# Routing an attention output to experts: 32x32 block transposes on VectorE in place of TensorE transposes, and rows scattered in quarters

## The chip, the cores and the metric

One core of a Trainium2 chip runs the whole program. The metric is the time of one execution in device microseconds. The engines are named as the profile names them: PE is TensorE (PEld its weight loads), DVE is VectorE, ACT is ScalarE, POOL is GpSimd, SP is SyncE.

## The reference

Squared-ReLU attention without a softmax, whose gated output goes token by token to one of eight experts.

```python
batch, seq, d_model, d_qk = 8, 2496, 256, 64          # attention
N, D, E, F = 19968, 256, 8, 1024                      # experts; N = 8 * 2496

scores = (1 / S) * z @ z.T                            # per batch
attn = np.maximum(scores, 0) ** 2
x = (u * (attn @ v)).reshape(N, D)

logits = x @ w_gate                                   # N x 8
e_idx = argmax(logits)                                # first of equals
probs = exp(logits - max); probs /= probs.sum() + 1e-9
gate_w = probs[e_idx]
eom = 1 / (1 + exp(-(x @ w_output_gate)))             # N x 8
for e in range(E):
    mask = e_idx == e
    h = np.maximum(x[mask] @ w1[e], 0)                # 256 -> 1024
    out[mask] = gate_w[mask] * eom[mask, e] * (h @ w2[e])   # 1024 -> 256
```

## The kernel before, in words

**Precision.** Every operand is kept as two float32r parts, a high part (a cast) and a low part (the operand minus its cast), and a product is two or three matmuls. So each operand needs a cast (ACT or DVE) and a subtraction (DVE).

**Attention.** The loop `for k, (b, c, jp) in enumerate(units)` runs over 8 batches, 5 chunks of columns `c` (512 wide, chunk 0 is 448) and 10 pairs `jp` of key blocks, one unit each. `make` prepares a unit two ahead (`LOOK = 2`): `scores` computes a block of the squared scores (matmuls at L200 and L201, ReLU at L202, square at L205, cast to `ah` at L207 on ACT for odd `jp` and at L209 on DVE for even, subtraction `al` at L211), and stores its transpose (DVE, L223 to L229) for later use; `take` fetches a transposed block that an earlier chunk stored (cast L255, subtraction L259). Chunk 0 has ten `scores` units and later chunks have ever more `take` units. `weigh` multiplies with `v` (twelve matmuls, L274) and accumulates two PSUM tiles `o` over the ten units.

**The tail.** When a chunk's ten units are done, a `Tail` finishes it: one call of `advance` in each unit of the next chunk, `TAIL = 11` steps, in this order. `gate` (DVE: times `u`), `split` (casts L314 on ACT, subtractions L315 on DVE), `rows(0)` and `rows(1)` (each: four PE transposes against an identity, L355, and two ACT copies out of PSUM, L364, into `xt`, four blocks of 128 tokens with 258 values each), `logits` (four matmuls with 32 weight columns, L325, an ACT copy `lg`, and for chunk 0 a POOL memset of the unused columns, L332), `turn` (four PE transposes, L338, an ACT copy `lt`), `choose` and `pick` (small DVE operations on 128 partitions x 4 blocks x 8 experts: the maximum, a one-hot row, a running count), `factor` and `finish` (gate weight and token number into the last two columns of `xt`), `place` (three small matmuls that count earlier tokens of the same expert) and `scatter` (small DVE operations that give the row index, then four indirect DMAs from POOL, L471, of 128 rows each, into the DRAM tensor `xs`, which has a region for each expert). PSUM bank `mp` (one buffer) serves all of the tail's PE results. The last tail has no next chunk: its steps are called from the list `later` during the first expert slots.

**Experts.** `Slot`s of 512 tokens (32 of them) and of 256 follow. A slot's table entry gives its expert and first row in `xs`. `load_x` reads the rows in four DMAs of 256-byte pieces, `turn` (DVE, L718) brings them into columns, `split_x` splits them, `split_w` splits the weights (L711 on ACT, L712 on DVE), `up` (L752, ReLU L761, L762) and `down` (L779) compute, and `down` writes `y` and scatters it to the output (POOL, L788). `then` is called after each of a slot's twelve parts (eight in `up`, four in `down`) and takes one entry of `later`. The first slots are cut so that they hold only tokens of the first seven batches, so they do not wait for the last batch's scatters.

**Order.** Each engine runs its instructions in the order in which the program writes them (`manual_schedule`). Tiles of one tag share its buffers, and a new tile waits for the last reader of the buffer that it is given.

Of the kernel before, what the change touches and what calls it, by code (L numbers as in the profile page):

```python
# [8 lines left out]
F32 = mybir.dt.float32  # L9
# [30 lines left out]
TAIL = 11  # L40

WARM = 10
ROW = D + 2
# [4 lines left out]
def attention_moe(ctx, tc, zt, zq_in, ut, v, wg, w12, out):  # L48
# [13 lines left out]
    xs = dram.tile([E * CAP + TW, ROW], F32, name="xs")  # L62
# [6 lines left out]
    ident = const.tile([P, P], F32, name="ident")  # L69
    make_identity(nc, ident)  # L70
    upper = const.tile([P, P], BF16, name="upper")
    nc.gpsimd.affine_select(
        out=upper, in_=ones, pattern=[[1, P]], compare_op=ALU.is_gt, fill=0.0, base=0, channel_multiplier=-1
    )
    ramp_i = const.tile([P, E], I32, name="ramp_i")
# [4 lines left out]
    tok_i = const.tile([P, 2, 4], I32, name="tok_i")  # L80
    nc.gpsimd.iota(tok_i[:, 0], pattern=[[P, 4]], base=0, channel_multiplier=1)
    for k in range(4):
        nc.gpsimd.iota(
            tok_i[k * 32 : (k + 1) * 32, 1],
            pattern=[[32, 4]],
            base=P * k,
            channel_multiplier=1,
        )
    tok0 = const.tile([P, 2, 4], F32, name="tok0")
    nc.vector.tensor_copy(out=tok0, in_=tok_i)  # L90
    scan_mask = const.tile([P, E, 5], BF16, name="scan_mask")
# [3 lines left out]
    for k in range(2):  # L95
        h = const.tile([P, E, 5], BF16, name=f"hot{k}")
        nc.vector.memset(h, 0.0)
        hot.append(h)
# [91 lines left out]
    def scores(b, c, jp):  # L190
# [15 lines left out]
        if jp % 2:  # L206
# [78 lines left out]
    class Tail:  # L285
# [33 lines left out]
        def logits(self):  # L319
            w = self.w  # L320
            lp = ps_m.tile([P, CH], F32, name="mp")
            k = 0
            for xx in (self.xl, self.xh):
                for d in range(2):
                    nc.tensor.matmul(  # L325
                        out=lp[0 : 4 * E, :w], lhsT=wg_r[:, d], rhs=xx[:, d, :w], start=k == 0, stop=k == 3
                    )
                    k += 1
            lg = pool.tile([4 * E, CH], F32, name="lg", bufs=1)
            nc.scalar.copy(out=lg[:, :w], in_=lp[0 : 4 * E, :w])  # L330
            if w < CH:
                nc.gpsimd.memset(lg[:, w:CH], 0.0)  # L332
            self.lg = lg

        def turn(self):
            tp = ps_m.tile([P, CH], F32, name="mp")
# [657 lines left out]
```

## Time and profile before

| | before |
|---|---|
| median of 3 runs | 2325.96 us (2324.8 to 2327.41) |
| profiled execution, its own time | 2326.99 us |
| its span | 2325.3 us |
| PE busy | 2301.2 us, 99% |
| DVE busy | 1629.2 us, 70% |
| ACT busy | 1499.9 us, 65% |
| POOL busy | 341.5 us, 15% |
| DMA traffic | 345.87 MB, mean 149 GB/s |

The span is what the profiler recorded from the first instruction to the last; the execution's own time is 1.7 us longer. The attention takes the first 1380 us, about 170.6 us a batch, and the experts the rest, 22.4 us for a slot of 512 tokens and 11.5 us for one of 256. An engine's busy time is the union of its instructions; matmuls are pipelined and their ends are modelled, so that neighbours overlap. In timelines a row gives the start, the duration, the engine, the line, the operation with output and inputs, and how many were merged.

### The profile page before, as it was taken

Reading aid. Unit: us, or ns where it says so; the run is one execution under the profiler, and the core shown is the slowest. Engines: PE = TensorE matmul, PEld = TensorE weight load, DVE = VectorE, ACT = ScalarE, POOL = GpSimd, SP = SyncE. Lnnn points to the kernel's source line nnn. Section 1 sums busy time; section 2 is a strip of 40 time slices with the busy share of each in tenths; the row PEclk is TensorE's granted clock in tenths of the full one; section 3 lists DMA queues with packets and bytes.
Section 4 is the critical chain, followed back from the end, with each engine's and each line's share of the span. In section 5 each row is a group of like instructions: output and inputs, shape, how many; then the busy total and the mean of one; then the engine's idle time right before and its main releaser. Section 6 shows DMA issues by size and latency. Waiting matters only on the chain.

```text
span 2325.3 us, 38469 instructions
## 1 busy us (share of the span) xinstructions
PE 2301.2 (99%) x12786; PEld 1992.8 (86%) x12786; DVE 1629.2 (70%) x2785; ACT 1499.9 (65%) x2503; POOL 341.5 (15%) x353
## 2 busy tenths in 40 slices
PE   9999999999999999999999999999999999999997
PEld 7888888888888888888888879999999999999997
DVE  8778778778778778777778666656556565566775
ACT  8767677777767767677677664555545455555664
POOL 0011011111011111111111112121111211111111
PEclk9999999999999999999999999999999999999999
DMA  6684674675765756756755675313322234445331
GB/s 202 177 213 154 188 200 169 187 186 180 194 168 189 203 156 201 204 150 193 199 150 189 183 185 140 87 46 85 89 78 51 82 83 127 139 122 157 106 96 42
DMA packets 393916, 345.87 MB, mean 149 GB/s; under 512 B 133869, under 2 KB 320238, under 8 KB 393712
## 3 DMA queue, kind: packets, MB, share of 16 engines
q1 hardware_dynamic: 378288, 302.29, 47.3%
q0 software_dynamic: 15424, 41.08, 5.2%
q8 instruction: 102, 1.67, 0.3%
q14 instruction: 102, 0.84, 0.1%
HBM read 272.55 MB, written 128.37 MB: 172 GB/s over the span
## 4 chain that ended last, share of the span: by engine, by line
PE 55%; issue 32%; POOL 7%; DVE 2%; DMA 2%; ACT 1%; POOLq 0%; SPq 0%; DVEq 0%; ACTq 0%
PE o L274 43%; POOL out L788 7%; PE sc L200 5%; PE sc L201 4%; PE mp L325 1%; PE mp L355 1%; DMA xs<-xt,idx 1%; PE mp L338 1%; DMA z<-td 0%; POOLq L788 0%; DVE t L226 0%; ACT a L202 0%; DMA sx<-xs 0%; ACT a L205 0%; PE o L779 0%
## 5 line engine op out<-in xcount | busy, mean ns | idle before, releaser
L274 PE MATMUL o<-ah,v 128*128 128x512 f32 (+1 forms) x3200 | 974.7, 388 | 1.5 <-DVE v L172 1.2
L274 PEld LDWEIGHTS o<-ah,v 128*128 128x128 f32 x3200 | 596.6, 188 | 114.0 <-DVE v L172 4.2
L274 PE MATMUL o<-al,v 128*128 128x512 f32 (+1 forms) x1520 | 586.7, 386 | 0.0
L779 PE MATMUL o<-w,hh 128*128 128x256 f32 x2624 | 480.5, 283 | 0.0
L779 PEld LDWEIGHTS o<-w,hh 128*128 128x128 f32 x2624 | 412.9, 192 | 1.2
L712 DVE TENSOR_TENSOR w<-raw,w 128x512 fp32r<-128x512 f32 x400 | 269.3, 685 | 194.9 <-ACT w L711 194.9
L211 DVE TENSOR_TENSOR al<-a,ah 128x1024 fp32r<-128x1024 f32 (+1 forms) x232 | 274.4, 1183 | 184.3 <-ACT ah L207 174.2
L752 PE MATMUL sc<-xh,w 128*128 128x512 f32 (+1 forms) x1600 | 376.4, 352 | 0.5 <-ACT xh L728 0.5
L779 PE MATMUL o<-w,hl 128*128 128x256 f32 x1312 | 371.9, 283 | 0.9 <-DVE hl L762 0.9
L471 POOL DMA_INDIRECT xs<-xt,idx x160 | 176.1, 1100 | 1229.0 <-DVE u L304 618.9
L202 ACT ACTIVATE a<-sc 128x512 f32<-128x512 f32 (+1 forms) x480 | 252.5, 580 | 155.5 <-PE sc L201 155.5
L274 PEld LDWEIGHTS o<-al,v 128*128 128x128 f32 x1520 | 285.8, 188 | 53.4
L752 PEld LDWEIGHTS sc<-xh,w 128*128 128x128 f32 x1600 | 270.8, 190 | 38.5 <-ACT xh L728 0.6
L761 ACT ACTIVATE hh<-sc 128x512 fp32r<-128x512 f32 x328 | 196.4, 599 | 122.8 <-PE sc L752 122.7
L788 POOL DMA_INDIRECT out<-y,meta x164 | 161.3, 984 | 741.9 <-ACT y L787 736.5
L787 ACT ACTIVATE y<-o,meta 128x256 f32<-128x256 f32 x164 | 77.8, 474 | 294.9 <-issue 195.7
L779 PEld LDWEIGHTS o<-w,hl 128*128 128x128 f32 x1312 | 251.9, 192 | 2.3 <-DVE hl L762 1.1
L205 ACT ACTIVATE a<-a 128x1024 f32<-128x1024 f32 (+1 forms) x240 | 246.2, 1026 | 7.6
L762 DVE SCALAR_TENSOR_TENSOR hl<-sc,hh 128x512 fp32r<-128x512 f32 x328 | 224.2, 684 | 35.1 <-ACT hh L761 24.6
L711 ACT CAST w<-raw 128x512 fp32r<-128x512 f32 x400 | 239.8, 614 | 0.0
L752 PE MATMUL sc<-xl,w 128*128 128x512 f32 (+1 forms) x800 | 216.2, 352 | 0.5 <-DVE xl L729 0.5
L200 PE MATMUL sc<-z,hl 128*128 128x512 f32 (+1 forms) x480 | 193.2, 403 | 1.7 <-ACT a L202 0.9
(132 smaller groups left out, 2281.7 us busy)
## 6 DMA issues: line engine op xcount, KB each, us to landing
raw<-in_w SPq DMA_DIRECT2D x400, 256.0 KB
td<-t SPq DMA_DIRECT2D x160, 512.0 KB
z<-td SPq DMA_DIRECT2D x640, 128.0 KB
raw<-in_v SPq DMA_DIRECT2D x72, 256.0 KB
u<-in_ut SPq DMA_DIRECT2D x32, 512.0 KB
sx<-xs SPq DMA_DIRECT2D x128, 128.0 KB
raw<-in_zt SPq DMA_DIRECT2D x40, 256.0 KB
raw<-in_zq SPq DMA_DIRECT2D x39, 256.0 KB
```

The lines of the kernel that those rows point to most:

```text
L200: nc.tensor.matmul(out=sc[:, :w], lhsT=st, rhs=ll[:, :w], start=True, stop=False)
L202: nc.scalar.activation(out=a[:, q, :w], in_=sc[:, :w], func=AF.Relu)
L205: nc.scalar.activation(out=a[:, :, :w], in_=a[:, :, :w], func=AF.Square)
L211: nc.vector.tensor_tensor(out=al[:, :, :w], in0=a[:, :, :w], in1=ah[:, :, :w].bitcast(F32), op=ALU.subtract)
L274: nc.tensor.matmul(out=o[d][:, :w], lhsT=vv[:, q, dd], rhs=rhs, start=begins and q == 0 and k == 0, stop=ends and q == 1 and k == len(term ...
L711: nc.scalar.copy(out=ww[:, 0], in_=wr)
L712: nc.vector.tensor_tensor(out=ww[:, 1], in0=wr, in1=ww[:, 0].bitcast(F32), op=ALU.subtract)
L752: nc.tensor.matmul(out=hp[:, at : at + n], lhsT=wb[2 * d + f // 4][:, ww, fs], rhs=xx[:, d, :], start=k == 0, stop=k == 5,)
L761: nc.scalar.activation(out=ho, in_=hp, func=AF.Relu)
L762: nc.vector.scalar_tensor_tensor(out=lo, in0=hp, scalar=0.0, in1=ho.bitcast(F32), op0=ALU.max, op1=ALU.subtract)
L779: nc.tensor.matmul(out=yp[:, :D], lhsT=hx[:, ts], rhs=wb[4 + f // 2][:, ww, ds_], start=k == 0, stop=k == 23,)
L788: it = nc.gpsimd.indirect_dma_start(out=out[:, :], out_offset=bass.IndirectOffsetOnAxis(ap=self.m.bitcast(I32)[:, q, 1:2], axis=0), in_=y, ...
```

## The change

The 32x32 block transpose of VectorE takes over what PE transposes did:

- The gate weights are laid out four times over (`wg_r` has 128 columns), so the logits matmul gives the same 32 logit rows in each group of 32 partitions. `turn` transposes them in 32x32 blocks straight from PSUM: each group of 32 partitions holds all 512 tokens, 32 by 16 blocks. All routing steps work on 128 partitions x 16 blocks instead of 128 x 4, the same values in four copies; the counting matmuls use a block-diagonal matrix `group`.
- `rows` is one block transpose of the gated columns. Each group of 32 partitions then holds a quarter (64 values) of every token's row, to which `finish` adds weight and token number: 66 values. `xs` has four such quarter rows for each token. `scatter` sends 16 indirect DMAs (14 for a chunk of 448) of 128 quarter rows, with index 4 x row + quarter, and none of them is ordered against another.
- `TAIL` is 10. The last tail's steps alternate with idle entries in `later`.
- In `scores`, the cast to `ah` is on ACT unless `jp` is a multiple of 4.
- A slot's four output blocks `y` are one tile, which shares its two buffers with `xr`. The first slot's `load_x`, `split_w`, `turn` and `split_x` come a unit earlier.

```diff
-TAIL = 11
+TAIL = 10
-ROW = D + 2
+
+NB = CH // 32
+
+SEG = D // 4 + 2
+ROW = 4 * SEG
@@ -59,41 +62,44 @@
-    xs = dram.tile([E * CAP + TW, ROW], F32, name="xs")
+    xs = dram.tile([(E * CAP + TW) * 4, SEG], F32, name="xs")
+    xs_rows = xs.rearrange("(n a) y -> n (a y)", a=4)
...
+
+    group = const.tile([P, P], BF16, name="group")
+    nc.vector.memset(group, 0.0)
+    for a in range(4):
+        nc.vector.memset(group[a * 32 : (a + 1) * 32, a * 32 : (a + 1) * 32], 1.0)
     upper = const.tile([P, P], BF16, name="upper")
     nc.gpsimd.affine_select(
-        out=upper, in_=ones, pattern=[[1, P]], compare_op=ALU.is_gt, fill=0.0, base=0, channel_multiplier=-1
+        out=upper, in_=group, pattern=[[1, P]], compare_op=ALU.is_gt, fill=0.0, base=0, channel_multiplier=-1
     )
...
-    wg_r = const.tile([P, 2, 4 * E], F32R, name="wg_r")
-    nc.vector.tensor_copy(out=wg_r[:, :, 0 : 2 * E], in_=wg_f)
-    nc.vector.tensor_tensor(
-        out=wg_r[:, :, 2 * E : 4 * E], in0=wg_f, in1=wg_r[:, :, 0 : 2 * E].bitcast(F32), op=ALU.subtract
-    )
+    wg_r = const.tile([P, 2, P], F32R, name="wg_r")
+    for a in range(4):
+        hi, lo = [wg_r[:, :, (4 * a + 2 * i) * E : (4 * a + 2 * i + 2) * E] for i in range(2)]
+        nc.vector.tensor_copy(out=hi, in_=wg_f)
+        nc.vector.tensor_tensor(out=lo, in0=wg_f, in1=hi.bitcast(F32), op=ALU.subtract)
@@ -203,7 +209,7 @@
         ah = act("ah")
         al = act("al")
         nc.scalar.activation(out=a[:, :, :w], in_=a[:, :, :w], func=AF.Square)
-        if jp % 2:
+        if jp % 4:
             nc.scalar.copy(out=ah[:, :, :w], in_=a[:, :, :w])
         else:
             nc.vector.tensor_copy(out=ah[:, :, :w], in_=a[:, :, :w])
 
         def logits(self):
             w = self.w
-            lp = ps_m.tile([P, CH], F32, name="mp")
+            lp = self.lp = ps_m.tile([P, CH], F32, name="mp")
             k = 0
             for xx in (self.xl, self.xh):
                 for d in range(2):
-                    nc.tensor.matmul(
-                        out=lp[0 : 4 * E, :w], lhsT=wg_r[:, d], rhs=xx[:, d, :w], start=k == 0, stop=k == 3
-                    )
+                    nc.tensor.matmul(out=lp[:, :w], lhsT=wg_r[:, d], rhs=xx[:, d, :w], start=k == 0, stop=k == 3)
                     k += 1
-            lg = pool.tile([4 * E, CH], F32, name="lg", bufs=1)
-            nc.scalar.copy(out=lg[:, :w], in_=lp[0 : 4 * E, :w])
+
+        def turn(self):
+
+            w = self.w
+            lt = pool.tile([P, NB, 2, 2 * E], F32, name="lt", bufs=1)
             if w < CH:
-                nc.gpsimd.memset(lg[:, w:CH], 0.0)
-            self.lg = lg
-
-        def turn(self):
-            tp = ps_m.tile([P, CH], F32, name="mp")
-            for q in range(4):
-                nc.tensor.transpose(
-                    out=tp[:, q * 32 : (q + 1) * 32],
-                    in_=self.lg[:, q * P : (q + 1) * P],
-                    identity=ident[0:32, 0:32],
-                )
-            lt = pool.tile([P, 4, 2, 2 * E], F32, name="lt", bufs=1)
-            nc.scalar.copy(out=lt.rearrange("p a b c -> p (a b c)"), in_=tp[:, 0:P])
+                nc.vector.memset(lt[:, w // 32 :], 0.0)
+            nc.vector.transpose(out=lt.rearrange("p n k i -> p (n k i)")[:, :w], in_=self.lp[:, :w])
             self.lt = lt
-        def rows(self, half):
-            if half == 0:
-                self.xt = pool.tile([P, 4, ROW], F32, name="xt", bufs=2)
-            tp = ps_m.tile([P, CH], F32, name="mp")
-            for qq in range(2):
-                q = 2 * half + qq
-                m = min(P, self.w - q * P)
-                for d in range(2):
-                    nc.tensor.transpose(
-                        out=tp[0:m, qq * D + d * P : qq * D + (d + 1) * P],
-                        in_=self.x[:, d, q * P : q * P + m],
-                        identity=ident,
-                    )
-
-            for qq in range(2):
-                q = 2 * half + qq
-                m = min(P, self.w - q * P)
-                nc.scalar.copy(
-                    out=self.xt[0:m, q, 0:D].rearrange("p (a k s) -> p k a s", a=4, k=2),
-                    in_=tp[0:m, qq * D : (qq + 1) * D].rearrange("p (k a s) -> p k a s", a=4, k=2),
-                )
+        def rows(self):
+
+            n = self.w // 32
+            self.xr = pool.tile([P, NB, SEG], F32, name="xr", bufs=2)
+            nc.vector.transpose(
+                out=self.xr[:, 0:n, 0 : D // 4].rearrange("p n (k s) -> p k n s", k=2),
+                in_=self.x[:, :, : self.w].rearrange("p k (n s) -> p k n s", s=32),
+            )
 
         def choose(self):
 
-            small = lambda name, shape=(P, 4, E): pool.tile(list(shape), F32, name=name)
-            l = small("l", (P, 4, 2 * E))
+            small = lambda name, shape=(P, NB, E): pool.tile(list(shape), F32, name=name)
+            l = small("l", (P, NB, 2 * E))
...
-            cand = small("cand")
+            cand = pool.tile([P, NB, E], F32, name="cand", tag="s8")
             if self.w < CH:
-                nc.vector.memset(hot_t[DQ:P, :, 4:5], 0.0)
-
-            cum = pool.tile([P, E, 5], BF16, name="cum")
+                nc.vector.memset(hot_t[:, :, self.w // 32 + 1 :], 0.0)
+
+            cum = pool.tile([P, E, NB + 1], BF16, name="cum")
...
-            nc.vector.reciprocal(out=self.xt[:, :, D : D + 1], in_=den)
+            nc.vector.reciprocal(out=self.xr[:, :, SEG - 2 : SEG - 1], in_=den)
             nc.vector.tensor_scalar(
-                out=self.xt.bitcast(I32)[:, :, D + 1 : D + 2],
+                out=self.xr.bitcast(I32)[:, :, SEG - 1 : SEG],
         def place(self):
 
             pp = ps_m.tile([P, CH], F32, name="mp")
-            pos = pp[:, 0:32].rearrange("p (e k) -> p e k", k=4)
-            nc.tensor.matmul(out=pos, lhsT=upper, rhs=self.hot[:, :, 1:5], start=True, stop=False)
-            nc.tensor.matmul(out=pos, lhsT=ones, rhs=self.cum[:, :, 0:4], start=False, stop=True)
-            nc.tensor.matmul(out=pp[:, 32:40], lhsT=ones, rhs=self.cum[:, :, 4], start=True, stop=True)
+            last = NB * E
+            pos = pp[:, 0:last].rearrange("p (e k) -> p e k", k=NB)
+            nc.tensor.matmul(out=pos, lhsT=upper, rhs=self.hot[:, :, 1:], start=True, stop=False)
+            nc.tensor.matmul(out=pos, lhsT=group, rhs=self.cum[:, :, 0:NB], start=False, stop=True)
+            nc.tensor.matmul(out=pp[:, last : last + E], lhsT=group, rhs=self.cum[:, :, NB], start=True, stop=True)
             self.pp, self.pos = pp, pos
...
-            at = pool.tile([P, 4, E], F32, name="at")
+            at = pool.tile([P, NB, E], F32, name="at", tag="s8")
-            mine = pool.tile([P, 4, E], F32, name="mine")
-            nc.vector.tensor_tensor(out=mine, in0=at, in1=self.oh, op=ALU.mult)
-            row = pool.tile([P, 4, 1], F32, name="row")
-            nc.vector.tensor_reduce(out=row, in_=mine, op=ALU.add, axis=AX.X)
-            idx = pool.tile([P, 4], I32, name="idx", bufs=2)
-            nc.vector.tensor_copy(out=idx, in_=row.rearrange("p a b -> p (a b)"))
-            for q in range(4):
-                m = min(P, self.w - q * P)
+            nc.vector.tensor_tensor(out=at, in0=at, in1=self.oh, op=ALU.mult)
+            row = pool.tile([P, NB, 1], F32, name="row")
+            nc.vector.tensor_reduce(out=row, in_=at, op=ALU.add, axis=AX.X)
+            idx = pool.tile([P, NB], I32, name="idx", bufs=2)
+            nc.vector.scalar_tensor_tensor(
+                out=idx, in0=row.rearrange("p a b -> p (a b)"), scalar=4.0, in1=quarter, op0=ALU.mult, op1=ALU.add
+            )
+            for n in range(self.w // 32):
                 it = nc.gpsimd.indirect_dma_start(
                     out=xs[:, :],
-                    out_offset=bass.IndirectOffsetOnAxis(ap=idx[0:m, q : q + 1], axis=0),
-                    in_=self.xt[0:m, q, :],
+                    out_offset=bass.IndirectOffsetOnAxis(ap=idx[:, n : n + 1], axis=0),
+                    in_=self.xr[:, n, :],
                     in_offset=None,
+                    bounds_check=(E * CAP + TW) * 4 - 1,
+                    oob_is_err=False,
                 )
-                if self.b == B - 1:
-                    tc.add_to_no_dep_group(last_scatters, it.ins)
+                group_of = last_scatters if self.b == B - 1 else "scatters"
+                for other in {"scatters", group_of}:
+                    tc.declare_no_dep(it.ins, group=other, reason="other rows")
+                tc.add_to_no_dep_group(group_of, it.ins)
             (
                 self.gate,
                 lambda: (self.split(0), self.split(1)),
-                lambda: self.rows(0),
-                lambda: self.rows(1),
+                self.rows,
                 self.logits,
...
 
         def down(self, then):
             wb = self.w
+            ys = pool.tile([P, 4, D], F32, name="y", tag="xr", bufs=2)
             for q in range(self.n // P):
-                y = pool.tile([P, D], F32, name="y", bufs=4)
+                y = ys[:, q]
                 yp = ps_o.tile([P, CH], F32, name="o")
@@ -857,6 +845,9 @@
         for k, (b, c, jp) in enumerate(units):
             pos = k % NPAIR
             make(k + LOOK)
+            if (b, c, pos) == (B - 1, NCH - 1, 8):
+                slots[0].turn()
+                slots[0].split_x()
@@ -874,20 +865,18 @@
                     slots[0].load_w(range(2 * pos - 2, 2 * pos + 2))
                 if c == NCH - 1 and 5 <= pos:
                     slots[1].load_w({5: (0, 1, 2), 6: (3,), 7: (4, 5), 8: (6,), 9: (7,)}[pos])
-                if c == NCH - 1 and pos in (6, 9):
+                if c == NCH - 1 and pos in (5, 9):
                     slots[pos // 9].load_x()
-                if c == NCH - 1 and pos >= 8:
-                    slots[0].split_w(range(2 * pos - 16, 2 * pos - 14))
-                if c == NCH - 1 and pos == 9:
-                    slots[0].turn()
-                    slots[0].split_x()
+                if c == NCH - 1 and 7 <= pos <= 8:
+                    slots[0].split_w(range(2 * pos - 14, 2 * pos - 12))
             if pos == NPAIR - 1:
                 tail = nxt
                 tails = [it for it in tails if it.step < TAIL] + [tail]
             prepare(k)
 
-    later = [tails[0].advance] + [tail.advance] * TAIL + [pads]
+    idle = lambda: None
+    later = [tails[0].advance] + [idle, tail.advance] * TAIL + [idle] * 8 + [pads]
     for steps_of in (full_table(1), rest_table()):
         later += [lambda it=steps_of: next(it, None)] * 6
```

Left out are changes of shape alone (4 blocks become `NB`, 16), constants, and the same view of `xs` by whole rows (`xs_rows`) in `pads` and `load_x`.

More of the change, by code (lines that the diff above doesn't have):

```diff
@@ L5 @@
 from concourse import mybir
-from concourse.masks import make_identity
 from concourse._compat import with_exitstack
@@ L78, in attention_moe @@
     nc.vector.tensor_copy(out=rank, in_=ramp_i)
[L80 to L87, printed above, removed]
-        )
-    tok0 = const.tile([P, 2, 4], F32, name="tok0")
+    tok_i = const.tile([P, 2, NB], I32, name="tok_i")
+    for a in range(4):
+        rows = tok_i[a * 32 : (a + 1) * 32]
+        nc.gpsimd.iota(rows[:, 0], pattern=[[32, NB]], base=0, channel_multiplier=1)
+        nc.gpsimd.iota(rows[:, 1], pattern=[[32, 4], [P, 4]], base=0, channel_multiplier=1)
+    tok0 = const.tile([P, 2, NB], F32, name="tok0")
     nc.vector.tensor_copy(out=tok0, in_=tok_i)
-    scan_mask = const.tile([P, E, 5], BF16, name="scan_mask")
+    scan_mask = const.tile([P, E, NB + 1], BF16, name="scan_mask")
     nc.vector.memset(scan_mask, 1.0)
@@ L95, in attention_moe @@
     for k in range(2):
-        h = const.tile([P, E, 5], BF16, name=f"hot{k}")
+        h = const.tile([P, E, NB + 1], BF16, name=f"hot{k}")
         nc.vector.memset(h, 0.0)
@@ L380, in pick @@
         def pick(self):
-            small = lambda name, shape=(P, 4, E): pool.tile(list(shape), F32, name=name)
+            small = lambda name, shape=(P, NB, E): pool.tile(list(shape), F32, name=name)
             dl, og = self.dl, self.og
@@ L411, in pick @@
             )
-            pick = small("pick")
+            pick = pool.tile([P, NB, E], F32, name="pick", tag="s8")
             nc.vector.tensor_tensor(out=pick, in0=oh, in1=og, op=ALU.mult)
-            osel = small("osel", (P, 4, 1))
+            osel = small("osel", (P, NB, 1))
             nc.vector.tensor_reduce(out=osel, in_=pick, op=ALU.add, axis=AX.X)
@@ L453, in scatter @@
             new = pool.tile([P, E], F32, name="carry", bufs=4)
-            nc.vector.tensor_tensor(out=new, in0=pp[:, 32:40], in1=old, op=ALU.add)
+            nc.vector.tensor_tensor(out=new, in0=pp[:, NB * E : NB * E + E], in1=old, op=ALU.add)
             carry[0] = new
-            at = pool.tile([P, 4, E], F32, name="at")
+            at = pool.tile([P, NB, E], F32, name="at", tag="s8")
             nc.vector.tensor_tensor(
@@ L672, in load_x @@
             n = self.n
[L673 removed]
+            rows = xs_rows[bass.ds(at, n), :]
             self.x = pool.tile([P, 2 * CH], F32, name="sx", tag="act", bufs=13)
@@ L685, in load_x @@
                 nc.sync.dma_start(
-                    out=self.m[:, 0 : n // P], in_=rows[:, D:ROW].rearrange("(q p) d -> p q d", p=P)
+                    out=self.m[:, 0 : n // P], in_=rows[:, SEG - 2 : SEG].rearrange("(q p) d -> p q d", p=P)
                 )
```

41 lines of the change are left out of this document (20 added, 21 removed).

## The prediction

> **What bounds the kernel now.** I read the page's busy table first, then busy time by stretch, the order of matmuls around one tail, the groups of instructions, and last whom TensorE waited for. The busy table:
>
> ```profile
> PE 2301.2 (99%) x12786; PEld 1992.8 (86%) x12786; DVE 1629.2 (70%) x2785; ACT 1499.9 (65%) x2503; POOL 341.5 (15%) x353
> ```
>
> Busy time by stretch (length, then busy PE, PEld, DVE, ACT, POOL, granted clock, DMA share, GB/s). The rows are: one batch of attention, its chunk 0, its chunk 1, the first batch's chunk 0, a chunk of the seventh batch, one expert slot.
>
> ```profile
> 353.70:524.30 170.60, 170.60 (x807) 140.68 (x806) 131.80 (x235) 123.14 (x196) 23.19 (x21) 1.00 0.66 185
> 353.70:386.50 32.80, 32.80 (x167) 29.50 (x166) 28.40 (x54) 25.91 (x43) 4.23 (x4) 1.00 0.52 183
> 386.50:421.00 34.50, 34.50 (x162) 27.91 (x161) 26.55 (x47) 26.67 (x41) 5.41 (x5) 1.00 0.61 183
> 12.60:46.00 33.40, 31.92 (x150) 27.22 (x149) 31.69 (x45) 28.73 (x45) 0.00 (x0) 1.00 0.56 189
> 1070.50:1105.00 34.50, 32.39 (x142) 26.02 (x141) 23.11 (x37) 24.06 (x38) 4.51 (x5) 0.95 0.62 184
> 1523.10:1545.50 22.40, 22.40 (x146) 20.51 (x145) 12.75 (x19) 11.67 (x22) 3.91 (x5) 1.00 0.21 48
> ```
>
> PE is busy for all 170.60 us of a batch; DVE is next (131.80), ACT 123.14. So a PE instruction that goes is worth its place in the stream, as long as DVE, which takes over the work, keeps up. Tightest is chunk 0: DVE 28.40 of 32.80 us.
>
> A busy PE counts overlapping matmuls, so I price the removed ones by starts (start, duration, instruction):
>
> ```profile
> 328.31 0.62 PE L274 MATMUL o<-ah,v 128*128 128x512 f32 x2
> 328.77 0.60 PE L355 MATMUL mp<-ident,u 128*128 128x128 f32 x4
> 329.13 0.48 PE L200 MATMUL sc<-z,hl 128*128 128x512 f32 x1
> 329.44 0.40 PE L201 MATMUL sc<-z,hl 128*128 128x512 f32 x1
> 329.68 0.39 PE L200 MATMUL sc<-z,hl 128*128 128x512 f32 x1
> ...
> 339.50 0.39 PE L274 MATMUL o<-al,v 128*128 128x512 f32 x1
> 339.81 0.43 PE L338 MATMUL mp<-ident,lg 32*128 32x32 f32 x4
> 340.18 0.73 PE L274 MATMUL o<-ah,v 128*128 128x512 f32 x2
> 340.74 0.40 PE L274 MATMUL o<-al,v 128*128 128x512 f32 x1
> ```
>
> A 512-column matmul holds the stream for 0.23 us (328.31 to 328.77 is two). From the first row transpose (328.77) to the second matmul after them (329.44) is 0.67 us; less one matmul, four transposes cost 0.44 us. A tail has two such fours: 0.88 us. For the turn, 339.50 + 0.23 to 340.74 is 1.01 us; less two matmuls, 0.55 us, a short wait for the logits' copy included. Together 1.43 us a tail.
>
> **The change part by part.** There are 8 x 5 = 40 tails, each stepped through the ten units of the next chunk (the last through the first expert slots). Prices:
>
> ```profile
> L211 DVE TENSOR_TENSOR al<-a,ah 128x1024 fp32r<-128x1024 f32 x160 | 196.1, 1226 | 164.0 <-ACT ah L207 156.2
> ...
> L223 DVE STREAM_TRANSPOSE t<-a 128x1024 f32<-128x1024 f32 x96 | 118.9, 1238 | 0.0
> ...
> L207 ACT CAST ah<-a 128x1024 fp32r<-128x1024 f32 x80 | 84.0, 1050 | 2.5
> ...
> L209 DVE CAST ah<-a 128x1024 fp32r<-128x1024 f32 x80 | 55.6, 695 | 31.1 <-ACT a L205 28.6 <-ACT eo L423 0.2
> ...
> L364 ACT COPY xt<-mp 128x256 f32<-128x256 f32 x152 | 49.4, 374 | 39.8 <-PE mp L355 39.8
> ...
> L718 DVE STREAM_TRANSPOSE xf<-sx 128x512 f32<-128x512 f32 x18 | 12.7, 703 | 0.0
> ```
>
> *Transposes off PE:* 40 x 1.43 = **-57.2 us**, all on the path.
>
> *Logits with 128 weight columns instead of 32:* the same four matmuls of 512. The weight load becomes as wide as those of L274, which sit behind a 0.23 us stream without widening it. I take 0; with that cover gone it would be 160 loads of at most 0.23 us, 37 us, and nothing in the stream of L274 shows such a thing.
>
> *Place:* two bf16 matmuls go from 32 to 128 columns. At 0.23 us per 512, 96 more columns are 0.04 us; twice, 40 tails: **+3.4 us** (0 if these are bound by their weight loads; 7 at double).
>
> *Rows and turn on DVE:* rows is one 128x1024 transpose, 1.24 us; turn is 128x512 read from PSUM. No row shows a transpose out of PSUM: the nearest from SBUF is 0.70 us, the other end is 1.24 us, and I take 0.70. Turn makes DVE wait for the logits on PE, and behind it stand the subtractions of L211 and L259. Its unit first issues the scores of two units later, which PE runs after those logits, and DVE has already subtracted them; so the wait has normally ended, and in units that only fetch DVE gives up no more than its lead.
>
> *Routing on four copies:* thirteen small operations grow from 32 to 128 elements, one from 64 to 256. L211 is 1.2 ns an element with its fixed part, so 14 x 96 x 1.2 ns = at most 1.6 us a tail; I take 1.5. DVE gains 1.24 + 0.70 + 1.5 = 3.4 us a tail.
>
> *Casts:* pairs 2 and 6 of chunks 0 and 1 and pair 6 of chunks 2 and 3 move: six a batch, 4.2 us off DVE, 6.3 us onto ACT. ACT loses four row copies (1.5 us) and the two logits' copies a tail, over 7.5 us a batch, so it ends no busier.
>
> DVE in a batch: 131.8 + 17.2 - 4.2 = 145 of a new 164 us. In chunk 0: 28.4 + 3.4 - 1.4 = 30.4 of 32.8 - 1.43 + 0.09 = 31.5 us, 97%. The trace has run at that: the first batch's chunk 0 has DVE at 31.69 of 33.40. Whom PE waited for (total us, times, longest us):
>
> ```profile
> PE mp L338 <- POOL lg L332: 2.1, 1, 2.1
> PE mp L841 <- DVE scan_mask L92: 1.4, 1, 1.4
> PE o L274 <- DVE v L172: 1.2, 2, 1.1
> ...
> PE mp L355 <- ACT xt L364: 0.8, 1, 0.8
> PE sc L200 <- DVE z L172: 0.8, 1, 0.8
> PE mp L355 <- PE sc L752: 0.7, 1, 0.7
> PE sc L752 <- DVE xl L729: 0.5, 1, 0.5
> PE sc L752 <- ACT xh L728: 0.5, 1, 0.5
> PE mp L355 <- DVE u L304: 0.3, 1, 0.3
> ```
>
> At 95% DVE cost PE 1.2 us there. Between 0 and 1.2 us for each of seven later chunk 0s I take 0.3, **+2 us**: a batch that runs in step has no start-up to catch up with.
>
> *The logits' clearing leaves POOL:* once PE waited 2.1 us because that memset stood behind a scatter, and the stretch around it (1070.50) ran at clock 0.95, 0.05 x 34.5 = 1.7 us more. The clearing is now on DVE: **-3.8 us**.
>
> *Start of the experts:* the last tail's transposes waited 0.8 + 0.7 + 0.3 us and go; slot 0's turn and split, 0.5 + 0.5 us late, come a unit earlier, their loads too: **-2.8 us**. The rows' new partner is the output tile y, which now shares two buffers with them. Slot 0's first y must wait until the tail before the last has sent 16 scatters, some 18 us from that chunk's last unit; PE goes on meanwhile, with four output banks. Slot 1's y is free if it gets slot 0's buffer; if it gets the last tail's, ACT stands behind 16 scatters issued just before, some 5 to 12 us beyond PE's cover. I take the first.
>
> *Scatters:* 16 issues a tail instead of 4, 14 for a short chunk. POOL's row (min/median/max ns):
>
> ```profile
> L471 POOL DMA_INDIRECT xs<-xt,idx x160: 898/961/1995, 90.5 to 1418.5; - x160
> ```
>
> 16 x 0.96 = 15.4 us, at the maximum 31.9 us, per chunk of 33 us: hidden, and xr has two buffers. They no longer wait for one another. For the DMA engines, the slot at 1523.10 moves 2048 pieces of 256 B, 512 of 8 B and 512 of 1 KB in 0.21 x 16 x 22.4 = 75 engine-us, 24 ns a piece; 2048 a tail are 49 of 540, so 0.66 becomes at most 0.75: hidden. SP gains no issue; slot 0's rows load one unit earlier, and the pads go out later than before, wanted only by the slots after the first 27.
>
> *Start:* six more small operations build the gate's weights on DVE, in its wait for the first keys: 0.
>
> **Sum:** 2326.99 (the profiled execution, 1.0 above the median) - 57.2 - 3.8 - 2.8 + 3.4 + 2 = 2268.6; as a median 2267.6. I say 2268.
>
> [...] PE lost clock after a 2.1 us wait (0.95 over 34.5 us). [...] POOL's longest scatter took 2.0 us against 0.96. [...]
>
> **The rivals.** *A: DVE binds chunk 0.* If transposing from PSUM or in this pattern costs 1.8 us more a tail, DVE needs 32.2 us of 31.5, 0.7 us late in each of eight chunks; if each also costs the clock 1.7 us, that is 19 us: 2266.6 + 19, about 2286. For: 97%. Against: 95% cost 1.2 us once.
>
> *B: scatters bind, slower.* From 32.9 / 16 = 2.05 us an issue, POOL no longer fits a chunk; xr stays full, DVE waits to write the next rows, PE behind it. At 3 us the chunk is 48 us, 15 more for 39 tails: about 2850. It passes the old time at 2.15 us. For: a maximum of 1.995. [...]
>
> *C: y waits for the last tail's scatters.* 5 to 12 us once: 2274 to 2280.
>
> *D: the place of the transposes is filled by something else (the weight loads of the logits, above, at 37 us, with A):* about 2325, no change.
>
> **How the numbers follow.** Forecast 0.70; A 0.14; C 0.08; B 0.06; D 0.02. Two in a thousand, 5 us, is what a measurement can tell. Faster: forecast, A and C, 0.92; same 0.02; slower 0.06. The forecast's own range is 2261 (place free, no lag, and the first chunk's 1.2 us gone) to 2274 (place doubled, 1.2 us a chunk lost). The range takes in C and A: 2259 to 2287.
>
> **What would show it.** A batch of 164 us instead of 170.6, PE still full, no L355 or L338 rows; DVE near 145 us a batch and 30 in chunk 0; the transpose from PSUM near 0.7 us; scatters near 1 us and 16 to a tail; no gap behind POOL. Wrong it is if PE waits for al in chunk 0, or for DVE's turn, if scatters pass 2 us, or if ACT stands still in slot 1.

## The result, and the profile after

The changed kernel takes 2267.05 us (median, 2264.89 to 2267.72), the kernel before beside it 2326.46: a ratio of 0.9744, interval 0.9727 to 0.9761. The forecast was 2268 us. The profiled execution took 2267.7 us, with a span of 2265.8 us against 2325.3. The mechanism was right, but that the total came out almost to the microsecond is luck: three parts were off and nearly cancel. Attention gained 60.2 us where the terms of the forecast add up to 55.6, the start of the experts cost 7.1 us where 2.8 were to be gained, and the end of the program gained 6.4 us that nobody had foreseen.

The busy table of the changed kernel, and the busy time of one batch of attention and of its chunk 0 (columns as in the prediction):

```profile
PE 2244.4 (99%) x12306; PEld 1965.8 (87%) x12306; DVE 1744.4 (77%) x2840; ACT 1472.5 (65%) x2311; POOL 925.8 (41%) x810
```

```profile
338.90:502.20 163.30, 163.30 (x747) 137.25 (x746) 146.19 (x239) 119.73 (x172) 95.53 (x78) 1.00 0.71 193
338.90:370.40 31.50, 31.50 (x157) 28.53 (x156) 28.93 (x48) 24.69 (x39) 19.24 (x16) 1.00 0.52 174
```

PE is still busy for the whole batch, with 60 matmul records fewer (12 transposes for each of five tails). DVE rose from 131.80 to 146.19 us, POOL from 23.19 to 95.53, and neither reached the batch's length.

The length of a batch can be read from two gates of the same chunk, one batch apart. First the kernel before, then the changed one (timeline of DVE: start, duration, instruction):

```profile
359.31 1.28 DVE L304 SCALAR_TENSOR_TENSOR u<-o,u 128x512 f32<-128x512 f32 x2
529.90 1.28 DVE L304 SCALAR_TENSOR_TENSOR u<-o,u 128x512 f32<-128x512 f32 x2
```

```profile
345.25 1.25 DVE L310 SCALAR_TENSOR_TENSOR u<-o,u 128x512 f32<-128x512 f32 x2
508.58 1.25 DVE L310 SCALAR_TENSOR_TENSOR u<-o,u 128x512 f32<-128x512 f32 x2
```

170.59 us became 163.33: 7.26 a batch, 1.45 us a tail. Whom PE waited for in the changed kernel, longest first:

```profile
PE sc L739 <- ACT xh L715: 2.6, 1, 2.6
PE sc L739 <- DVE hl L749: 2.6, 2, 1.6
PE sc L739 <- DVE w L699: 1.9, 1, 1.9
...
PE o L280 <- DVE al L217: 0.4, 1, 0.4
```

The wait for `al`, which rival A would have made the longest, is 0.4 us in all. The large ones are in L739, the first matmuls of an expert slot. So I cut the span at two landmarks: the first matmul of slot 0 and the first of the last slot (timeline of PE; in brackets the idle time before it). Before:

```profile
1379.24 0.73 PE L752 MATMUL sc<-xh,w 128*128 128x512 f32 x2 [0.52 <-ACT xh L728]
...
2299.93 0.40 PE L752 MATMUL sc<-xh,w 128*128 128x256 f32 x2
```

After:

```profile
1321.15 0.50 PE L739 MATMUL sc<-xh,w 128*128 128x512 f32 x1 [2.61 <-ACT xh L715]
1323.60 0.80 PE L739 MATMUL sc<-xh,w 128*128 128x512 f32 x1 [1.95 <-DVE w L699]
...
2246.83 0.40 PE L739 MATMUL sc<-xh,w 128*128 128x256 f32 x2
```

PE leaves attention where that first wait begins: at 1378.72 before and 1318.54 after, -60.2 us. From there to the last slot it took 921.2 us and now 928.3, +7.1. From the last slot to the end of the span it took 25.4 us and now 19.0, -6.4. The sum is -59.5 us, the difference of the two spans.

### The profile page after: what moved, and what is told of

The parts are those of the page before. It is cut to its first block, busy times and chain, and to the rows that moved or that the text cites. A ratio compares the mean times of both kernels' runs of the same rounds, so it can differ in the third digit from the quotient of the medians.

```text
span 2265.8 us, 38207 instructions
## 1 busy us (share of the span) xinstructions
PE 2244.4 (99%) x12306; PEld 1965.8 (87%) x12306; DVE 1744.4 (77%) x2840; ACT 1472.5 (65%) x2311; POOL 925.8 (41%) x810
## 4 chain that ended last, share of the span: by engine, by line
PE 53%; issue 33%; POOL 8%; DVE 2%; DMA 2%; ACT 1%; POOLq 0%; SPq 0%; DVEq 0%; ACTq 0%
PE o L280 43%; POOL out L776 7%; PE sc L206 4%; PE sc L207 4%; PE mp L331 1%; POOL xs L455 1%; DMA z<-td 1%; DVE al L217 1%; DMA sx<-xs 0%; DMA xs<-xr,idx 0%; POOLq L776 0%; DVE t L229 0%; DMA raw<-in_w 0%; DVE t L232 0%; ACT a L208 0%
## 5 line engine op out<-in xcount | busy, mean ns | idle before, releaser
L455 POOL DMA_INDIRECT xs<-xr,idx x624 | 762.3, 1222 | 614.9 <-DVE idx L451 425.6
L739 PE MATMUL sc<-xh,w 128*128 128x512 f32 (+1 forms) x1600 | 378.8, 353 | 7.3 <-ACT xh L715 2.6
L739 PEld LDWEIGHTS sc<-xh,w 128*128 128x128 f32 x1600 | 271.8, 190 | 47.9 <-DVE hl L749 4.3
L739 PE MATMUL sc<-xl,w 128*128 128x512 f32 (+1 forms) x800 | 217.0, 353 | 0.5 <-DVE xl L716 0.5
L206 PE MATMUL sc<-z,hl 128*128 128x512 f32 (+1 forms) x480 | 184.0, 383 | 3.0 <-ACT a L208 1.8
```

Of the source, the lines that this page charges most:

```text
L206: nc.tensor.matmul(out=sc[:, :w], lhsT=st, rhs=ll[:, :w], start=True, stop=False)
L455: it = nc.gpsimd.indirect_dma_start(out=xs[:, :], out_offset=bass.IndirectOffsetOnAxis(ap=idx[:, n : n + 1], axis=0), in_=self.xr[:, n, :] ...
L739: nc.tensor.matmul(out=hp[:, at : at + n], lhsT=wb[2 * d + f // 4][:, ww, fs], rhs=xx[:, d, :], start=k == 0, stop=k == 5,)
```

## The experiments

**1. The transposes back on PE, unread.** Does the gain come from PE's stream?

```diff
 # Tail.rows, behind the block transpose on VectorE
+tp = ps_m.tile([P, CH], F32, name="mp")
+for q in range(4):            # eight of the gated columns
+    for d in range(2):
+        nc.tensor.transpose(out=tp[...], in_=self.x[:, d, q*P : q*P+m], identity=ident)
+for q in range(4):            # four of 32x32
+    nc.tensor.transpose(out=tp[0:P, q*32:(q+1)*32], in_=self.x[0:32, 0, ...], identity=ident[0:32, 0:32])
```

> The changed kernel, with twelve TensorE transposes a tail put back (eight of 128x128 from the gated columns, four of 32x32) into a tile that nothing reads; the block turns on VectorE stay. Theory (attention is one TensorE stream, and what was gained is its time in that stream): 40 x (8 x 0.11 + 4 x 0.11) = 52.8 us longer, 2320 us (2314 to 2326); a batch goes from 163.3 back to about 170 us. Rival (the gain came from the casts, from the clearing that left POOL, from scatters that no longer wait for one another, or from the order at the start of the experts): those are all kept here, so the time stays within 6 us of 2267 us. In between, the part that is back is the part that TensorE's stream had given.

Measured: 2321.4 us, ratio to the kernel before 0.9979 (0.997 to 0.9988), 54.3 us above the changed kernel. Two gates of it, one batch apart:

```profile
358.38 1.25 DVE L313 SCALAR_TENSOR_TENSOR u<-o,u 128x512 f32<-128x512 f32 x2
528.96 1.25 DVE L313 SCALAR_TENSOR_TENSOR u<-o,u 128x512 f32<-128x512 f32 x2
```

170.58 us: the batch of the kernel before, to 0.01 us, with all else of the change in place. The twelve transposes thus cost 7.25 us a batch, 1.45 a tail. Over eight batches that is 58.0 us; the total shows 3.7 less. Only 39 of the 40 tails run within attention, where PE loses 56.0 us by the trace, and slot 0's first matmul now starts without the wait of 2.6 us.

**2. VectorE's room.** Three kernels with more work on DVE.

```diff
 # casts_half and dve_full
-if jp % 4:
+if jp % 2:
 # dve_twice and dve_full: both block turns of a tail a second time, into the same place
+nc.vector.transpose(out=self.xr[...], in_=self.x[...])
+nc.vector.transpose(out=lt[...], in_=self.lp[:, :w])
```

> The changed kernel, with every second cast on VectorE again instead of every fourth: six casts a batch of 0.70 us, 4.2 us, go back to VectorE, and two of them, 1.4 us, fall into chunk 0 of each batch. Theory (VectorE and ScalarE both have room behind TensorE): VectorE is busy 141 of 163.3 us a batch and 30.3 of 31.5 us in chunk 0, and the time stays within 3 us of 2267 us. Rival (the casts had to move, since VectorE is at its limit in chunk 0): PE waits for al in seven or eight chunks and the time rises by 5 to 20 us, 2272 to 2287.

> The changed kernel, with both new block turns of a tail done twice into the same place: 1.22 + 0.70 = 1.92 us more a tail on VectorE, 77 us in all. This is the extra 1.8 us a tail of rival A of the prediction. In chunk 0 VectorE is then at 28.93 + 1.92 = 30.85 of 31.5 us by the busy time that was measured. Theory (VectorE has that room): 2267 to 2272 us, no waits of PE for al in attention. Rival A (at this price VectorE binds chunk 0, and each late chunk also costs clock): 19 us more, about 2286 us.

> The changed kernel, with both of these: every second cast on VectorE again, and both block turns done twice. In chunk 0 that is 28.93 + 1.40 + 1.92 = 32.25 us of VectorE work in 31.5 us of TensorE work; in a batch 137.3 + 4.2 + 9.6 = 151 of 163.3 us. Theory (VectorE binds only from the point where its work in a chunk exceeds that of PE, and it carries some lead into the chunk): 0 to 0.75 us late in each of eight chunks, 2267 to 2275 us. Rival A with its price for the clock: 8 x (0.75 + 1.7) = 20 us, 2287 us. Rival (VectorE is hidden whatever it does as long as the batch as a whole fits): 2267 us within 2 us.

DVE's share of a batch in these expectations starts from 137.3 us, which is PEld's time in the changed kernel's batch; DVE's is 146.19, and with the edits 150.1, 154.9 and 159.2 us were measured.

Measured: 2267.0 us with the casts (ratio 0.9745, 0.9732 to 0.9758), 2276.5 with the turns doubled (0.9788, 0.9774 to 0.9801), 2290.2 with both (0.9845, 0.9831 to 0.9858). The casts' move brought nothing. The doubled turns cost 9.5 us, which neither theory had. Both together cost 23.2, near rival A's 20, but not for its reason: the granted clock stays at 1.00 through the longer batch. Waits of PE with the turns doubled, and with both, and a batch with both:

```profile
PE o L280 <- DVE al L217: 7.4, 9, 1.1
```

```profile
PE o L280 <- DVE al L217: 12.7, 24, 1.4
```

```profile
208.81:375.07 166.26, 164.34 (x745) 137.16 (x745) 159.20 (x256) 113.61 (x166) 94.61 (x78) 1.00 0.73 190
```

The place is chunk 0, as the prediction had it: with the turns doubled, a wait stands at the end of chunk 0 of every batch but the first, 0.9 us each time, 6.0 of the 7.4 us. The third batch's:

```profile
372.83 0.47 PE L280 MATMUL o<-al,v 128*128 128x448 f32 x1 [0.86 <-DVE al L217]
```

From this wait to the next batch's it is 164.6 us on average over the batches, against 163.3: 1.2 us a batch. With both edits the wait at this place is 0.86 us again, although DVE has 1.4 us more to do in the chunk; the batch loses 2.9 us, with further small waits in other places. So the chunk's sum of work does not give the lateness. In the changed kernel, the same place looks like this (first DVE, then PE):

```profile
368.82 1.08 DVE L217 TENSOR_TENSOR al<-a,ah 128x896 fp32r<-128x896 f32 x1
```

```profile
369.96 0.47 PE L280 MATMUL o<-al,v 128*128 128x448 f32 x1
```

`al` is done at 369.90 and its matmul starts 0.06 us later, and so in all seven later batches (0.05 to 0.06 us): no wait, but hardly any room either, though DVE is only 92% busy in that chunk. What idle time DVE has there is waiting for casts `ah` that are on ACT: 0.90 us before the gate, and behind it

```profile
356.51 1.09 DVE L217 TENSOR_TENSOR al<-a,ah 128x896 fp32r<-128x896 f32 x1 [0.27 <-ACT ah L213]
359.74 1.09 DVE L217 TENSOR_TENSOR al<-a,ah 128x896 fp32r<-128x896 f32 x1 [0.33 <-ACT ah L213]
```

This is how the casts' 1.4 us can cost nothing: where DVE makes the cast itself, it no longer waits for ACT's, and these 1.5 us of waits are gone from that kernel's trace. The doubled turns are work of another kind. They stand behind the gate, where 0.6 us of DVE's time was free: 1.92 - 0.60 = 1.3 us (an estimate from these rows) against the 1.2 us that were lost.

**3. Scatters in order.**

```diff
-group_of = last_scatters if self.b == B - 1 else "scatters"
-for other in {"scatters", group_of}:
-    tc.declare_no_dep(it.ins, group=other, reason="other rows")
-tc.add_to_no_dep_group(group_of, it.ins)
+if self.b == B - 1:
+    tc.add_to_no_dep_group(last_scatters, it.ins)
```

> The changed kernel, with its 16 scatters a tail ordered as they were before the change (each waits until the one ahead of it has landed); only those of the last batch stay free of the order towards slot 0's rows and the pads. A scatter of the changed kernel takes 1.09 us and lands 4.4 us after its issue (medians). Theory (POOL's cover rests on the scatters being unordered): 78 scatters a batch x some 4.9 us = 382 us against 163.3 of TensorE, so POOL binds, the time is about 8 x 382 + 950 = 4000 us (3000 to 4500), and PE waits behind DVE's write of xr. Rival (the order cost little before, and costs little now; the scatters are hidden either way): 2267 to 2280 us.

Measured, in a single run: 3035.7 us. POOL's scatters there (ns min/median/max), and DVE's longest wait:

```profile
L455 POOL DMA_INDIRECT xs<-xr,idx x624: 964/969/2022, 84.6 to 2160.9; - x156
```

```profile
DVE xr L347 <- DMA xs<-xr,idx: 712.1, 36, 31.7
```

POOL's queue binds, and PE waits behind DVE's write of xr, as expected. The size was overrated: (2160.9 - 84.6) / 624 = 3.3 us a scatter, not 4.9, since a scatter alone lands sooner (2.3 us after its issue, median) than among others (4.4 us in the changed kernel). One batch, from gate to gate:

```profile
483.66:742.97 259.31, 174.97 (x747) 144.50 (x746) 146.36 (x240) 119.68 (x172) 86.39 (x78) 0.83 0.45 122
```

That is rival B of the prediction at a price of 259.31 / 78 = 3.3 us: 259.3 - 163.3 = 96 us a batch, 768 for eight, 3035 us. That the total agrees so well is in part luck: 707.6 us are lost before the first slot, and 60.6 behind it. The chain of rival B, from scatters that no longer fit to DVE and PE, is what this run shows; its cause, a longer issue, is not: the median issue is 0.97 us, and POOL waits for landings, 1365.3 us in 617 waits. In the changed kernel POOL is busy for 95.53 of 163.30 us, and the missing order is what keeps it there.

**4. The clearing alone, in the kernel before.**

```diff
-nc.gpsimd.memset(lg[:, w:CH], 0.0)
+nc.vector.memset(lg[:, w:CH], 0.0)
```

> The kernel before the change, with only the clearing of the logits' unused columns moved from POOL to VectorE. The prediction's step: PE's one wait of 2.1 us behind that clearing and the clock that it cost, 1.7 us, go: 2326.3 - 3.8 = 2322.5 us. Rival (the wait moves to what is late next, or VectorE's extra 0.1 us a batch counts): 2326 us within 1. Its trace also gives a second sample of what comes after the last slot: the kernel before spent 25.4 us from the start of its last slot to its end, five kernels with the change 18.97 to 18.99 us. If 25.4 stands here, that difference belongs to the change; if 19, it is a matter of chance.

Measured: 2323.07 us beside 2326.74, ratio 0.9983 (0.9974 to 0.9992): -3.7 us. It is one batch, the seventh. Its two gates in the kernel before, then here:

```profile
1041.64 1.28 DVE L304 SCALAR_TENSOR_TENSOR u<-o,u 128x512 f32<-128x512 f32 x2
1216.09 1.28 DVE L304 SCALAR_TENSOR_TENSOR u<-o,u 128x512 f32<-128x512 f32 x2
```

```profile
1041.61 1.28 DVE L304 SCALAR_TENSOR_TENSOR u<-o,u 128x512 f32<-128x512 f32 x2
1212.19 1.28 DVE L304 SCALAR_TENSOR_TENSOR u<-o,u 128x512 f32<-128x512 f32 x2
```

174.45 us became 170.58, the length of the others.

**5. The end.** The difference behind the last slot is a matter of the last steps of POOL. The closing lines' drains of POOL (ns min/median/max), in the kernel before and in the changed one:

```profile
L990 POOLq DRAIN  x3: 40/107/8885, 2315.6 to 2325.0; - x3
```

```profile
L979 POOLq DRAIN  x3: 40/107/3822, 2261.2 to 2265.6; - x3
```

```diff
 # the kernel before, its scatters
+bounds_check=E * CAP + TW - 1,
+oob_is_err=False,
```

> The kernel before the change, with only the bound on the index of each scatter that the changed kernel has. It is for what stands behind the last output: the kernel before and the one with the clearing moved spent 25.4 and 25.7 us from the start of the last slot to the end, 8.88 us of it POOL's last drain; every kernel with the change 19.0 to 19.2 us, with 3.82 to 4.04 us of drain. Theory (the bound selects another form of the scatter, and POOL has less to finish): 19 us there, and 2326.5 - 6.4 = 2320 us. Rival (it is the number of scatters, 160 against 624, or their place in the program): 25.4 us there, and 2326 us, or up to 3 us more for the longer scatter.

Measured: 2326.57 us beside 2326.53, ratio 1.0001 (0.9992 to 1.001), and the drain takes 8885 ns as before. The bound is not it. The kernel with the clearing moved has 8885 too; the one with the transposes back has 3822, those with ordered scatters and with y elsewhere 4.0 and 3.9 us. So it belongs to the change, and neither to the clearing, nor to the scatters' missing order, nor to y's place, nor to the transposes. The rest, the number of scatters (160 or 624) and the rows' new shape above all, was not told apart.

**6. The start of the experts.** Two things came late there: slot 0's rows, and ACT, which stood 9.6 us for the buffer of slot 0's first y:

```profile
1310.27 3.00 SPq L666 DMA_DIRECT2D sx<-xs  x4
```

```profile
ACT y L775 <- DMA xs<-xr,idx: 9.6, 1, 9.6
```

```diff
 # y_act
-ys = pool.tile([P, 4, D], F32, name="y", tag="xr", bufs=2)
+ys = pool.tile([P, 4, D], F32, name="y", tag="act", bufs=13)
 # x_early: slots[0].load_x() at pos 3 instead of 5, ahead of the loads of that unit
```

> The changed kernel, with the output tile y in the buffers of the h tiles (thirteen) instead of sharing two with the scattered rows. Theory (in slot 0 ACT waits 9.6 us to write y, since the buffer is held by the scatters of the tail before the last, and the splits of slot 1 stand behind it): that wait goes, slot 1's start comes 2.5 us earlier (26.3 us between the starts of slots 1 and 2 becomes 23.8), and the time falls by 2.5 to 3.5 us to about 2264 us. Rival (PE's delays there come from VectorE, which is behind with the last tail and the weights, and not from ACT): within 1 us of 2267 us.

> The changed kernel, with slot 0's rows asked for two units earlier, ahead of the second half of slot 0's weights. Theory (the rows land too late: SP issues them at 1310.3 us and PE waits 2.6 us for xh, then 1.95 us for a weight split that stands behind the late turn on VectorE): the first wait goes and the second shrinks, 2.5 to 4.5 us, to about 2264 us. Rival (whatever is moved ahead in SP's queue makes a weight or a block of z late instead): 2267 us or more.

Measured: 2285.8 us (ratio 0.9827, 0.9814 to 0.9841) and 2285.0 us (0.9824, 0.9811 to 0.9838): 18 to 19 us slower than the changed kernel, against both theories. The two lose in the same places, slots 0 and 2. ACT's h tiles in slot 2, with the rows early and then in the changed kernel:

```profile
1389.67 0.60 ACT L748 ACTIVATE hh<-sc 128x512 fp32r<-128x512 f32 x1 [4.58 <-remote]
1395.32 0.60 ACT L748 ACTIVATE hh<-sc 128x512 fp32r<-128x512 f32 x1 [4.54 <-PE sc L739]
```

```profile
1380.32 0.60 ACT L748 ACTIVATE hh<-sc 128x512 fp32r<-128x512 f32 x1 [0.25 <-PE sc L739]
1381.67 0.60 ACT L748 ACTIVATE hh<-sc 128x512 fp32r<-128x512 f32 x1 [0.25 <-PE sc L739]
```

In `up`, six matmuls make one tile, and it comes every 5.65 us instead of every 1.35, four times as slow. Busy time by stretch there (the eighth column is the granted clock):

```profile
1383.00:1391.00 8.00, 2.86 (x12) 1.70 (x10) 1.99 (x4) 2.21 (x4) 6.15 (x7) 1.00 0.08 25
1391.00:1399.00 8.00, 5.06 (x12) 3.45 (x12) 1.90 (x3) 1.10 (x2) 5.41 (x7) 0.52 0.21 75
```

Twelve matmuls in 8 us, first at a recorded clock of 1.00: nothing that the profile shows holds PE. The last two matmuls of one tile and the first two of the next, in the kernel with the rows early:

```profile
1386.40 0.62 PE L739 MATMUL sc<-xh,w 128*128 128x512 f32 x2
1391.05 1.04 PE L739 MATMUL sc<-xh,w 128*128 128x512 f32 x2 [4.02 <-issue]
```

The six starts of a tile stand as close as elsewhere (1385.37 to 1386.63), and then comes a gap of 4 us. But ACT got that tile only at 1389.67, and matmul ends are modelled, so the rows do not say whether PE ran slowly or stood still. What brought the tiles to a quarter of their pace was not shown. Since both kernels had run on one chip, on which the changed kernel had not, the next three ran together on another.

```diff
 # w_early and xw_early (xw_early has x_early's edit as well)
-if c == NCH - 1 and 7 <= pos <= 8:
-    slots[0].split_w(range(2 * pos - 14, 2 * pos - 12))
+if c == NCH - 1 and pos == 7:
+    slots[0].split_w(range(4))
```

> The changed kernel, unaltered, on the chip of the three kernels beside it. Two runs that moved one thing at the start of the experts (the output tile, or slot 0's rows) were 18 us slower, both at the same places: PE fell to half clock in slots 0 and 2. Theory (the changed kernel stands at an edge there, and small moves push it over): 2267 us here again, and slot starts 29.9, 26.3, 22.4 us apart. Rival (it depends on the chip that a kernel runs on): the changed kernel may show 2285 us here as well, and slot starts 35, 25, 36 us apart.

> The changed kernel, with all four first weight splits of slot 0 in the last unit but two, where VectorE stands idle for 4 us, instead of two of them behind slot 0's turn. Theory (PE's second wait at the start, 1.95 us for that split, is VectorE's order): it goes, and the time is that of the unaltered kernel beside it less 2 to 3 us (2264 to 2265, if that shows 2267). Rival (the rows land late, and the wait for them only grows by what the other wait gives): no change.

> Both moves: slot 0's rows asked for two units earlier, and its first four weight splits ahead of its turn. Theory (edge): as slot 0's rows alone, 2285 us, less at most 3. Rival (chip): the unaltered kernel's time on this chip less 4 to 6 us, since both first waits of PE, 2.6 and 1.95 us, go.

Measured: the unaltered kernel 2265.8 us (ratio 0.9742, 0.9729 to 0.9755), the weight splits earlier 2263.9 (0.9734, 0.9721 to 0.9747), both moves 2266.0 (0.9742, 0.9728 to 0.9755). With the rows early the 18 us do not appear here, so they do not come from that move alone. Whether the chip or the moment decides stays open, as the unaltered kernel was not run on that chip. Experiment 3's kernel was, and it has no such place: slot 1 takes 26.4 us there, and the tiles of slot 2 come every 1.36 us. `y` in the h tiles was run on that chip only, so its theory is untested. The earlier splits do what they should: 2.0 us by the medians, and PE's first matmuls of slot 0 go through but for 0.53 us:

```profile
1318.28 0.73 PE L739 MATMUL sc<-xh,w 128*128 128x512 f32 x2
1319.54 0.73 PE L739 MATMUL sc<-xl,w 128*128 128x512 f32 x2 [0.53 <-DVE xl L716]
```

It is the fastest version found, by a margin that the runs barely separate from the changed kernel (intervals overlap). Beside it, asking for the rows early as well costs 2.1 us. They are then issued at 1301.22 instead of 1308.04, but PE still waits 2.01 us for xh: slot 0's turn stands on DVE behind a block of z, whose cast on ACT waited 6.27 us for its transfer, against 4.41 with the splits alone. So the late rows are not the only cause of the first wait. The unaltered order shows such a wait for z too (6.41 us in the profile of the changed kernel), so it is not shown that the move made the block late.

## Why the prediction was right, and where it was not

- *Transposes off PE, -57.2 us:* right, in size and cause. 1.43 us a tail were read off matmul starts, 1.45 was measured, and experiment 1 gives the batch back to 0.01 us.
- *Logits with 128 weight columns at 0, place at +3.4 us:* both about right, read off the starts. Place's three matmuls held the stream for 0.09 us and now for 0.16 (one tail, before from 352.87 to 352.96, after from 369.25 to 369.41; the others agree): 0.07 us a tail, +2.7 in all. The logits' four went from 0.92 to 0.93 us. The batch with the transposes back contains both and is still no longer than before's; it lacks the short wait that the turn had before, which may make up for place.
- *DVE:* 145 us a batch was forecast, 146.19 came; in chunk 0 it was 30.4, and 28.93 came (29.49 in a stretch cut 0.8 us later). The routing is the part mis-sized: its operations on DVE, summed from the two profiles, took 3.5 us a tail before and 5.7 now, +2.2 instead of +1.5. Turn and rows came at their prices:

```profile
L347 DVE STREAM_TRANSPOSE xr<-u 128x1024 f32<-128x1024 f32 (+1 forms) x40 | 47.6, 1191 | 0.0
L382 DVE TENSOR_TENSOR hot<-cand,best 128x128 bf16<-128x128 f32 x40 | 28.6, 715 | 1.4
L340 DVE STREAM_TRANSPOSE lt<-mp 128x512 f32<-128x512 f32 (+1 forms) x40 | 27.1, 677 | 0.0
```

- *Lag in chunk 0, +2 us:* not there. No later chunk 0 waits. But it is close: experiment 2 shows a matmul that starts 0.06 us after DVE is done with its operand. The prediction judged the room by DVE's busy share, which does not give it: the casts' 1.4 us in chunk 0 cost nothing, and 1.9 us of turns cost 1.2 us a batch.
- *POOL's clearing, -3.8 us:* right; -3.7 alone.
- *Casts:* hidden, as said, and without use: the change would be as fast without them.
- *Scatters:* hidden, as said. Once they are ordered, in experiment 3, what rival B describes happens. No run shows the 3 us an issue at which rival B was priced: the medians were 0.97 to 1.16 us, and with the order 3.3 us from one scatter to the next, landing included.
- *Start of the experts, -2.8 us:* wrong, +7.1. The step that failed is "slot 0's turn and split come a unit earlier, their loads too". The load is a unit earlier in the order, but SP is behind: it issued the rows 8.3 us before PE left attention (1310.27 against 1318.54), while before it was 10.9 us (1367.79 against 1378.72):

```profile
1367.79 2.64 SPq L679 DMA_DIRECT2D sx<-xs  x4
```

  DVE turned slot 0's rows at 1318.77, 0.2 us after PE had left attention, where before it did so 1.9 us ahead. It had waited 1.46 us for the rows, and before that 4.09 us behind the cast of a block of z that landed late too. What made both late was not found. Two weight splits stood behind the late turn, the 1.95 us that experiment 6 took away, and in the profiled run the clock fell there (0.77 from 1318 to 1326 us, 0.80 to 1334).

  The prediction's other sentence, that PE "goes on meanwhile" while slot 0's y waits, overlooked who stands behind ACT: ACT waited 9.6 us, until 1349.59, for the scatters of the tail before the last, and the split of slot 1's rows followed at 1349.97. DVE waited 8.6 us for it and then fell behind with the last tail's routing, and PE waited for its parts. From the first matmul of slot 1 to that of slot 2 went 23.8 us before and 26.3 now; 2.5 us, not rival C's 5 to 12. This is rival C's mechanism in another slot, read from one trace; no run took the wait away without other losses. Of the +7.1, the first wait is 2.1, slot 0 is 1.4, slot 1 is 2.5, and 1.0 in slot 3 is not explained.
- *The end, not foreseen, -6.4 us:* POOL's last drain is 5.1 us of it.

Together: -60.2 at the end of attention (forecast: -57.2, -3.8, +3.4 and +2, that is -55.6), +7.1 (forecast -2.8) and -6.4 (forecast 0). The errors are -4.6, +9.9 and -6.4, and they nearly cancel. The range was right, but a kernel with an unchanged end would have shown 2273.

## What to carry to other kernels

When one engine is busy through a whole stage, an instruction off it is worth its distance between starts, not its duration (here the starts gave 1.43 us a tail, the mean durations add up to 8 x 273 + 4 x 228 ns = 3.1 us, and 1.45 was measured), and putting the instructions back unread shows it: the batch returned to 0.01 us. Before shifting work to another engine, find its edge with doubled work, and do not read it off the busy share: here DVE was 92% busy in a chunk and had no room left for more turns at its end, yet took casts at no cost, because it had been waiting for them. A shared buffer is also a wait for everybody behind the engine that writes it (here ACT waited 9.6 us for it, and DVE 8.6 us for ACT): list what stands behind, and look at a queue's real issue time instead of its place in the order (here 8.3 us before PE left attention instead of 10.9, for a load that was written a unit earlier).

## What the runs showed of the hardware

The granted clock fell behind some waits of about 2 us and not behind others of the same length. The unaltered kernel of experiment 6 first, its two waits of PE at the start of slot 0, with busy time by stretch:

```profile
1320.34 0.50 PE L739 MATMUL sc<-xh,w 128*128 128x512 f32 x1 [1.39 <-ACT xh L715]
1322.79 0.50 PE L739 MATMUL sc<-xh,w 128*128 128x512 f32 x1 [1.95 <-DVE w L699]
```

```profile
1319.00:1327.00 8.00, 4.71 (x20) 3.68 (x21) 6.36 (x17) 4.78 (x9) 1.84 (x2) 1.00 1.10 269
```

Then the kernel with casts and doubled turns of experiment 2, which has the second of these waits alone:

```profile
1344.48 0.50 PE L744 MATMUL sc<-xh,w 128*128 128x512 f32 x1 [1.95 <-DVE w L704]
```

```profile
1341.00:1349.00 8.00, 6.05 (x19) 4.41 (x19) 6.51 (x16) 4.09 (x7) 1.94 (x2) 0.80 1.08 234
```

One wait of 1.95 us left the clock at 1.00, even behind one of 1.39; behind the other it was 0.80 over 8 us, and 0.50 in its lowest 2 us (1346 to 1348). That is about 3.2 us at half clock, a loss of 1.6 us (an estimate from these rows). Waits of 2.01 us (both moves of experiment 6) and 2.28 us (slot 1 of its unaltered kernel) came with 0.79 over 8 us. Why the clock fell behind some of these waits and not behind others was not shown.

A comparison that writes 128 bf16 values in the strided order of hot takes 715 ns (L382 above), while float operations of the same size beside it take 275 to 292, one 409; which of type, order and operation makes it slow was not told apart. And the length of a scatter differs between these kernels. The changed kernel's:

```profile
L455 POOL DMA_INDIRECT xs<-xr,idx x624: 969/1088/2036, 84.0 to 1388.7; - x156
```

That is a median of 1.09 us. With six casts a batch moved back to DVE it is 1.16, with the turns doubled 1.03, and with both 1.06, while kernels that leave DVE's attention work as it is give 1.06 to 1.11; in the ordered kernel, where a scatter has no others beside it, it is 0.97. DVE's busy time alone does not order these: the doubled turns add to it (155 of 165 us a batch), and the scatters got no longer. With the casts the median was higher both times, by 0.07 and 0.03 us, beside 0.05 us between the kernels that leave DVE's attention work as it is; what makes a scatter longer was not told apart.
